# Bridging the last expert into the first dense tile with one-hot products, with wider row products and another split between VectorE and ScalarE

## The chip, the cores and the metric

One core of a Trainium2 chip runs the kernel. The metric is the device time of one launch in microseconds (us); the figure of a kernel is the median of its runs.

## The reference

Three layers run one after the other; all inputs are random, the dense weights come as 64-bit floats.

```
# 1: a complex decaying state, 4 batches x 8 heads x 768 steps, head size 48
a = a * min(|a|, 0.999) / (|a| + 1e-6)
S = a[t][:, None] * S + outer(k[t], v[t]);   y[t] = q[t] @ S.re
# 2: tokens x (3072 x 384); a token is computed if x @ w_skip > 0
e = argmax(x @ w_gate);   gate = softmax(x @ w_gate)[e]
x[token] += gate * (relu(x[token] @ w1[e]) @ w2[e])     # 8 experts, 384 -> 1024 -> 384
# 3: dense, 384 -> 2048 -> 384
h = x @ w_in;   out = max(0.01 * h, h) @ w_out
```

## The kernel before, in words

The batch is cut into two units of two batches (1536 tokens, `UT`). For each unit the work goes through the same stages:

1. *Rows* (`attention_rows`): on 128 rows (batch, head, chunk of 96 steps) VectorE normalises `a` (`norm`), runs the running product `P` step by step (`steps`: a product `t` and a sum `P` for each of the 96 steps, each needing the one before), and scales `q` and `k` by it (`scaled`). Steps come in blocks of 4 to 8 (unit 0) or 3 to 6 (unit 1). In unit 0 the order of a block on VectorE, ScalarE and TensorE is written out by hand: `timed` gives every instruction a place in the block from the `AT_...` lists, and the engines keep that order. Unit 0's products stay on the chip in two large tiles called `stash` (k and q).
2. *Chunks* (`attention_chunks`): 16 pairs of chunk and batch on TensorE. In unit 0 `columns` turns k's columns back into rows (`kps`, into `kqt`): the copy of one half of the heads goes to ScalarE, of the other to VectorE.
3. *Routing* (`Routing.part`, in two parts of 14 and 2 pairs): which 128 tokens each expert takes (`idx`), and their gates (`gsl`).
4. *Experts* (`Experts`): for each of 8 experts the tokens' rows are gathered from the DRAM buffer `xd` (`gathers`, one indirect DMA each), turned (`columns`), multiplied by `w1` (`first`, four groups), then by `w2` (`second`), gated and added to the token's row on VectorE (tile `xo`), and scattered back to `xd` by an indirect DMA on GpSimd.
5. *Dense* (`Dense`): tiles of 512 tokens (`TN`). `load` reads the tile's rows from `xd` into `xr` (SyncE's DMA queue), `columns` turns them by 12 TensorE transposes in three groups and splits each group into two fp16 halves (`xTh` by ScalarE, `xTl` by VectorE), `first` makes 16 slices of the hidden layer with 9 matmuls each, `second` makes the output. Two tiles run between unit 0's experts and unit 1's chunks.

Unit 1's rows (`behind`) and the conversion of the dense weights (`convert`) are fillers. A filler is a generator; `budget(gen, us, engines)` draws instructions from it until the costs that it yields reach `us`. `BG_CHUNK` is drawn at each of the 80 yields of unit 0's chunks, `BG_ROUTE` after the routing, and `BG_EXPERT` four times in each expert as long as the expert's number is below `LASTE`. `convert` takes `w_in` in 16 pieces: a piece of 64-bit words is loaded into one of two `raw` buffers (its DMA is issued when the piece before the last has been read), VectorE packs it in three instructions (`cst`), ScalarE makes the high half and VectorE the low half (`m2w`). `swap`, after expert 3's `first`, puts the conversion of `w_in` ahead of the rows in the experts' filler `feed`; what is left of it is run after the experts. `w_out` is converted while the first dense tile runs.

The program's scheduler may move an instruction ahead of others on its engine by its own estimate of when operands are ready. Where `keep("V")` (or A, T, G) is on, an instruction is instead queued behind the one that was written just before it on that engine. `budget(..., "VA")` turns this on for the filler's VectorE and ScalarE instructions in the experts; in the dense stage the rows are drawn without it. SyncE's DMA queue issues in order: an issue that has to wait holds those behind it.

A filler's cost for one instruction over n steps is `(70 + 1.04 * n * 48) / 1e3`, for one of a conversion `(70 + 1.04 * 384) / 1e3`.

## Time and profile before

| what | us |
|---|---|
| median of 3 runs (921.21 to 929.61) | 927.39 |
| profiled execution | 919.73 |
| its span | 917.6 |
| TensorE busy | 820.6 (89%) |
| VectorE busy | 608.4 (66%) |
| ScalarE busy | 502.4 (55%) |
| GpSimd busy | 140.5 (15%) |

The span is one execution from its first to its last instruction; times in the rows below are from the span's start. The profile gives the engines short names: PE is TensorE's matmul, PEld its weight load, DVE VectorE, ACT ScalarE, POOL GpSimd, SPq and ACTq the DMA queues of SyncE and ScalarE. "Busy" of an instruction runs from its start to its end, and two in a row can overlap.

In that execution unit 0's rows run until about 134 us, its chunks until about 215, the routing until 238, the experts until 328, then comes a gap on TensorE, then the two dense tiles from 346 to 480. Unit 1's chunks start at 480, its experts and the other dense tiles fill the rest.

### The profile page before, as it was taken

How to read it: one execution, taken by the hardware profiler on the slowest of the kernel's cores; microseconds unless marked ns; L12 is line 12 of the kernel's file. 1: busy time of each engine (PE TensorE's matmuls, PEld its weight loads, DVE VectorE, ACT ScalarE, POOL GpSimd, SP SyncE). 2: the span in 40 equal slices, each digit the busy share in tenths (PEclk: the TensorE clock that was granted, in tenths of full speed). 3: DMA queues.
4: the chain of work that ended last, by engine and by line, in shares of the span. 5: the costliest groups of instructions: out<-in, count | busy, mean ns of one | idle time of the engine just before them, and what ended most of it. 6: DMA issues, size and time to landing. Idle time of an engine off the chain costs nothing.

```text
span 917.6 us, 17826 instructions
## 1 busy us (share of the span) xinstructions
PE 820.6 (89%) x6674; PEld 569.8 (62%) x6674; DVE 608.4 (66%) x1534; ACT 502.4 (55%) x1071; POOL 140.5 (15%) x162
## 2 busy tenths in 40 slices
PE   2888878997699939999999979989999999999997
PEld 1666667997488814545569978547686546456454
DVE  6999974787999988999803654876676460450530
ACT  5789875675456445646507866565564350440530
POOL 9100012121714330000022111140111000000000
PEclk9999999999799978999999999999999999999999
DMA  5567536898589976364357995064773201000000
GB/s 153 149 173 197 158 101 192 261 271 283 191 283 331 321 230 223 105 207 136 95 146 185 247 260 153 21 206 154 242 238 111 85 5 57 10 1 26 9 10 28
DMA packets 126512, 143.61 MB, mean 157 GB/s; under 512 B 34058, under 2 KB 109514, under 8 KB 126416
## 3 DMA queue, kind: packets, MB, share of 16 engines
q1 hardware_dynamic: 113488, 120.46, 43.9%
q10 hardware_dynamic: 10880, 17.30, 5.8%
q0 software_dynamic: 2048, 4.61, 1.4%
q8 instruction: 54, 0.88, 0.4%
q14 instruction: 42, 0.34, 0.1%
HBM read 115.62 MB, written 28.41 MB: 157 GB/s over the span
## 4 chain that ended last, share of the span: by engine, by line
PE 52%; DVE 18%; DMA 15%; ACT 10%; issue 3%; SPq 1%; ACTq 0%; POOLq 0%; POOL 0%; DVEq 0%
PE ops L91 18%; PE hps L91 12%; PE yps L91 6%; PE sps L91 4%; DVE gg L91 4%; PE ad L91 3%; DVE cst L91 3%; DVE gl L91 3%; DMA cw<-in_moe_w_dram 2%; ACT gh L91 2%; PE tps L91 2%; DMA raw<-in_moe_w_in_dram 2%; DMA kqt<-kqd 2%; DMA vt<-vd 2%; PE ups L91 2%
## 5 line engine op out<-in xcount | busy, mean ns | idle before, releaser
L91 PE MATMUL hps<-xTh,m2w 128*128 128x512 f16 x576 | 173.8, 381 | 1.0 <-DVE gg L91 0.8
L91 PEld LDWEIGHTS <-m2w 128*128 128x128 f16 x864 | 84.6, 98 | 101.3 <-issue 4.4
L91 PE MATMUL ops<-m2w,gh 128*128 128x384 f16 x512 | 125.2, 326 | 0.0
L91 PE MATMUL hps<-xTl,m2w 128*128 128x512 f16 x288 | 109.4, 381 | 0.2 <-DVE xTl L91 0.2
L91 DVE TENSOR_TENSOR gg<-hps,gg 128x512 f32<-128x512 f32 x96 | 65.6, 684 | 65.2 <-ACT gg L91 64.9
L91 PE MATMUL ops<-m2w,gl 128*128 128x384 f16 x256 | 83.5, 326 | 0.0
L91 ACT ACTIVATE ot<-ops 128x384 f32<-128x384 f32 x24 | 11.6, 489 | 125.9 <-PE ops L91 125.9
L91 PEld LDWEIGHTS <-gh 128*128 128x128 f16 x512 | 50.1, 98 | 32.7
L91 ACT ACTIVATE gg<-hps 128x512 f32<-128x512 f32 x96 | 56.3, 587 | 20.7 <-PE hps L91 13.8
L91 PE MATMUL ops<-m2w,stash 128*128 128x384 f16 x384 | 65.3, 326 | 2.5 <-ACT m2w L91 1.7
L91 DVE TENSOR_TENSOR t<-P,a 128x192 f32<-128x192 f32 x190 | 66.5, 350 | 0.9 <-DVE kr L91 0.3
L91 DVE TENSOR_TENSOR gl<-gg,gh 128x512 f16<-128x512 f32 x64 | 44.2, 690 | 33.9 <-ACT gh L91 33.2
L91 DVE SCALAR_TENSOR_TENSOR w<-cw,w 128x768 f16<-128x768 f32 x64 | 59.7, 952 | 9.3 <-ACT w L91 8.4
L91 ACT ACTIVATE gh<-gg 128x512 f16<-128x512 f32 x64 | 40.2, 629 | 42.8 <-DVE gg L91 42.7
L91 ACT ACTIVATE w<-cw 128x768 f16<-128x768 f32 x64 | 53.0, 842 | 18.6 <-DMA cw<-in_moe_w_dram 16.1
L91 POOL TENSOR_SCALAR_AFFINE_SELECT sc<-sc 96x384 f32<-96x384 f32 x64 | 34.8, 552 | 159.9 <-ACT sc L91 159.5
L91 POOL DMA_INDIRECT xd<-xo,idx x16 | 35.3, 2204 | 155.0 <-DVE xo L91 113.0
L91 PEld LDWEIGHTS <-stash 128*128 128x128 f16 x384 | 37.5, 98 | 29.7 <-issue 5.1
L91 DVE TENSOR_TENSOR P<-t 128x96 f32<-128x96 f32 x190 | 48.0, 253 | 1.4
L91 PE MATMUL yps<-stash,hh 128*128 128x384 f32 x128 | 42.8, 487 | 0.0
L91 PE MATMUL yps<-sc,vt 128*64 128x96 f32 x512 | 41.6, 251 | 0.0
L91 ACT ACTIVATE hh<-hps 128x256 f32<-128x256 f32 (+1 forms) x64 | 23.7, 378 | 30.8 <-PE hps L91 26.2
(243 smaller groups left out, 1724.8 us busy)
## 6 DMA issues: line engine op xcount, KB each, us to landing
cw<-in_moe_w_dram SPq DMA_DIRECT2D x64, 384.0 KB
stash<-in_moe_w_dram ACTq DMA_DIRECT2D x16, 768.0 KB
stash<-in_moe_w_dram SPq DMA_DIRECT2D x16, 768.0 KB
kqt<-kqd SPq DMA_DIRECT2D x16, 576.0 KB
kqd<-kq SPq DMA_DIRECT2D x14, 576.0 KB
vd<-gv SPq DMA_DIRECT2D x32, 192.0 KB
vt<-vd SPq DMA_DIRECT2D x32, 192.0 KB
raw<-in_moe_w_in_dram SPq DMA_DIRECT2D x16, 384.0 KB
```

What stands on the lines that cost most here:

```text
L91: ins = getattr(self.engine, op)(*args, **kw)
```

## The change

- The first dense tile's rows are loaded after expert 6 (`tiles`), before expert 7's result is in `xd`. GpSimd and VectorE make a one-hot matrix of 128 slots by 512 tokens from expert 7's token list (an iota of 384 and one of 128 columns, two comparisons). Expert 7's gated result is first made alone (`yg`), `Dense.columns` accumulates on its transposes, now written as products with the identity, the product of `yg` with the one-hot matrix (two matmuls in each of the three groups), and only then the row sum `xo` is made and scattered. From expert 6 on the VectorE instructions of `second` keep the written order.
- `LASTE` goes from 7 to 8: expert 7 draws fillers too. What is left of `w_in`'s conversion keeps its order on VectorE.
- In unit 0's rows three products that were made in halves (two in `scaled`, one in `norm`) are made in one instruction each; `AT_NORM` and `AT_SCALED` lose the places of the halves.
- `columns` of unit 0's chunks copies both halves of `kps` by ScalarE.
- `BG_CHUNK` goes from 0.3 to 0.4, and while a routing part is being drawn in unit 0's chunks, the rows are not drawn after it.

```diff
-BG_CHUNK = 0.3
+BG_CHUNK = 0.4
-BG_EXPERT, LASTE = 2.0, 7
+BG_EXPERT, LASTE = 2.0, 8
-AT_NORM = (0.034, 0.118, 0.189, 0.26, 0.342, 0.381)
+AT_NORM = (0.034, 0.118, 0.189, 0.26, 0.381)
-AT_SCALED = (0.481, 0.525, 0.746, 0.75, 0.862, 0.93, 0.961)
+AT_SCALED = (0.481, 0.746, 0.75, 0.862, 0.93)
...
-            if stash:
-                V.tensor_tensor(kq[1][:, :, 0], kq2[:, 1], P[:, :, 0], ALU.mult)
-                yield cost(i)
-                V.tensor_tensor(kq[1][:, :, 1], kq2[:, 1], P[:, :, 1], ALU.mult)
-            else:
-                V.tensor_tensor(kq[1], both(kq2[:, 1], i), P, ALU.mult)
+            V.tensor_tensor(kq[1], both(kq2[:, 1], i), P, ALU.mult)
...
-                if a:
-                    V.tensor_copy(half, p)
-                else:
-                    A.activation(half, p, AF.Copy)
+                A.activation(o["kqt"][:L, 4 * a:4 * a + 4, 0, :], p, AF.Copy)
...
-        def second(self, e):
+        def second(self, e, early=None):
...
-            V.scalar_tensor_tensor(xo, yps, gsl[self.ui][:, e:e + 1], self.xg[e], ALU.mult, ALU.add)
+            keep("V" if self.place and e >= E - 2 else "")
+            if early:
+                yg = self.xp.tile([128, DM], F32, tag="xo", name="yg")
+                V.tensor_scalar(yg, yps, gsl[self.ui][:, e:e + 1], None, ALU.mult)
+                early(yg)
+                V.tensor_tensor(xo, yg, self.xg[e], ALU.add)
+            else:
+                V.scalar_tensor_tensor(xo, yps, gsl[self.ui][:, e:e + 1], self.xg[e], ALU.mult, ALU.add)
+            keep("")
             scatter(xd[self.ui], xo, idx[self.ui][:, e:e + 1], UT)
...
                 for s in range(4):
-                    T.transpose(tp_[:, s, :], self.xr[:, s, kk * 128:(kk + 1) * 128], ident)
+                    if late:
+                        T.matmul(tp_[:, s, :], self.xr[:, s, cs], ident, start=(s == 0), stop=False)
+                    else:
+                        T.transpose(tp_[:, s, :], self.xr[:, s, cs], ident)
+                for n, (ts, oh) in enumerate(late[1] if late else ()):
+                    T.matmul(tp_.rearrange("p s t -> p (s t)")[:, ts], late[0][:, cs], oh, start=False, stop=n > 0)
...
-            budget(first_of(todo + [gen]) if todo else gen, us, "VAT")
+            budget(first_of(todo + ([] if ck.stash else [gen])) if todo else gen, us, "VAT")
...
+    def tiles():
+        dense.extend(Dense(u, t, mlp2["x"], None if u or t >= ND else g) for u in range(NU) for t in range(UT // TN))
+        dense[0].load()
+        oh = [ex.xp.tile([128, DM], F32, tag=f"xg{i}", name="oh", bufs=1) for i in range(2)]
+        at = oh[1][:, TN - DM:TN - DM + 1]
+        V.tensor_copy(at, idx[0][:, E - 1:E])
+        for x, n, t in ((oh[0], DM, 0), (oh[1], TN - DM, DM)):
+            G.iota(x[:, :n], pattern=[[1, n]], base=t, channel_multiplier=0, allow_small_or_imprecise_dtypes=True)
+            V.tensor_scalar(x[:, :n], x[:, :n], at, None, ALU.is_equal)
+            late.append((slice(t, t + n), x[:, :n]))
+
+    then[E - 2, 1] = tiles
+    experts(ex, feed, BG_EXPERT, then=then, early=lambda yg: dense[0].columns((yg, late)))
...
+    keep("V")
     run(mlp2["conv", 0])
...
-    dense[0].load()
-    dense[0].columns()
```

## Rows read from the trace of the kernel before

**Rows 1.** By stretch: busy PE, PEld, DVE, ACT, POOL (instructions), clock, DMA share, GB/s

```profile
60.00:80.00 20.00, 16.97 (x126) 12.83 (x126) 19.69 (x59) 18.04 (x44) 0.00 (x0) 1.00 0.63 178
180.00:200.00 20.00, 20.00 (x314) 19.14 (x314) 16.00 (x47) 14.37 (x34) 4.84 (x8) 1.00 0.97 279
```

**Rows 2.** The chain that ended last, 282 to 352 us: start, us, what

```profile
288.14 6.24 DMA raw<-in_moe_w_in_dram
...
296.17 5.29 DMA raw<-in_moe_w_in_dram
...
335.29 6.47 DMA xd<-xo,idx
...
341.78 4.44 DMA xr<-xd
...
346.26 1.97 PE tp L91 x8
```

**Rows 3.** Timeline around the gap, all engines: start, us, what, wait and its releaser

```profile
314.31 1.60 SPq L859 DMA_DIRECT2D stash<-in_moe_w_dram  x2
...
321.04 0.61 DVE L91 SCALAR_TENSOR_TENSOR xo<-yps,gsl,xg 128x384 f32<-128x384 f32 x1
...
322.90 5.56 PE L91 MATMUL yps<-stash,hh 128*128 128x384 f32 x16
...
334.41 0.61 DVE L91 SCALAR_TENSOR_TENSOR xo<-yps,gsl,xg 128x384 f32<-128x384 f32 x1
...
335.29 4.35 POOL L91 DMA_INDIRECT xd<-xo,idx  x1 [10.93 <-DVE xo L91]
...
340.82 0.36 DVE L91 TENSOR_SCALAR cst<-raw 128x384 int32<-128x384 int32 x1 [1.51 <-DMA raw<-in_moe_w_in_dram]
```

**Rows 4.** Timeline, VectorE in one block of unit 0's rows: start, us

```profile
59.91 0.36 DVE L91 TENSOR_TENSOR t<-P,a 128x192 f32<-128x192 f32 x1
60.30 0.26 DVE L91 TENSOR_TENSOR P<-t 128x96 f32<-128x96 f32 x1
60.48 0.55 DVE L91 TENSOR_TENSOR pu<-ad,pg 128x384 f32<-128x384 f32 x1
60.95 0.35 DVE L91 TENSOR_TENSOR t<-P,a 128x192 f32<-128x192 f32 x1
61.21 0.55 DVE L91 SCALAR_TENSOR_TENSOR pu<-pu,pg 128x384 f32<-128x384 f32 x1
```

**Rows 5.** Timeline, VectorE in unit 1's rows and where the conversion of w_in starts

```profile
258.16 0.75 DVE L91 TENSOR_TENSOR a<-ari,nrr 128x576 f32<-128x576 f32 x1
258.83 0.35 DVE L91 TENSOR_TENSOR t<-P,a 128x192 f32<-128x192 f32 x1
...
267.38 0.75 DVE L91 TENSOR_TENSOR a<-ari,nrr 128x576 f32<-128x576 f32 x1
...
285.77 0.61 DVE L91 SCALAR_TENSOR_TENSOR xo<-yps,gsl,xg 128x384 f32<-128x384 f32 x1
286.30 0.35 DVE L91 TENSOR_SCALAR cst<-raw 128x384 int32<-128x384 int32 x1
```

**Rows 6.** Copies of the tile kps: ns min/median/max, first and last start

```profile
L91 ACT ACTIVATE kqt<-kps x16: 472/480/502, 135.6 to 213.9; 96x384 f32<-96x384 f32 x16
L91 DVE COPY kqt<-kps x16: 541/547/554, 136.3 to 215.7; 96x384 f32<-96x384 f32 x16
```

**Rows 7.** The scatters of xd alone: ns min/median/max, first and last start

```profile
L91 POOL DMA_INDIRECT xd<-xo,idx x16: 969/1318/8409, 260.3 to 711.6; - x16
```

**Rows 8.** The tile cst alone, 5 us stretch: DVE busy (instructions), ACT, clock, DMA, GB/s

```profile
385.00:390.00 5.00, 3.14 (x8) 1.05 (x2) 1.00 0.49 164
```

**Rows 9.** Waits between 346 and 482 us: in total, times, longest

```profile
PE ops L91 <- ACT m2w L91: 1.7, 1, 1.7
```

**Rows 10.** Timeline, end of unit 1's rows and start of its chunks

```profile
456.06 0.36 SPq L313 DMA_DIRECT2D kqd<-kq  x1
...
480.54 3.32 PE L91 MATMUL tps<-ident,kqt 96*96 96x96 f32 x32
```

More of the change, by code (lines that the diff above doesn't have):

```diff
@@ L243, in norm @@
             a4s[i] = a4
[L244 to L249 removed]
+            V.tensor_tensor(a4[:, :, 0::2, :], ari.rearrange("p c t d -> p t c d"), both(rr, i), ALU.mult)
             if i + 3 < nb and not (stash and i in MIRROR):
@@ L301, in scaled @@
             yield cost(i)
-            if stash:
-                V.tensor_tensor(kq[0][:, :, 0], kq2[:, 0], P[:, :, 0], ALU.mult)
-                yield cost(i)
-                V.tensor_tensor(kq[0][:, :, 1], kq2[:, 0], P[:, :, 1], ALU.mult)
-            else:
-                V.tensor_tensor(kq[0], both(kq2[:, 0], i), P, ALU.mult)
+            V.tensor_tensor(kq[0], both(kq2[:, 0], i), P, ALU.mult)
             if i + 2 < nb:
@@ L967, in load, with columns @@
                               .rearrange("(s p) c -> p s c", p=128))
-        def columns(self):
+        def columns(self, late=None):
             self.xTh = self.xp.tile([128, 3, TN], F16, tag="xTh", name="xTh2", bufs=1)
@@ L1160, in second_ff, with experts @@
                 yield 2
-    def experts(ex, behind, us, then={}, mixed=none):
+    def experts(ex, behind, us, then={}, mixed=none, early=None):
         if ex.place:
@@ L1258, in moe_attention_kernel @@
     then[3, 0] = swap
-    experts(ex, feed, BG_EXPERT, then=then)
+    room = stash[0].rearrange("p c b t -> p (c b t)").bitcast(F16)
+    g = [room[:, j * 16 * TN:(j + 1) * 16 * TN].rearrange("p (f t) -> p f t", f=16) for j in range(2)]
+    dense, late = [], []
+    def tiles():
[10 more added lines that the diff above has]
+    experts(ex, feed, BG_EXPERT, then=then, early=lambda yg: dense[0].columns((yg, late)))
     (wih, wil), (woh, wol), m2x = mlp2[0], mlp2[1], mlp2["x"]
@@ L1262, in moe_attention_kernel @@
     ex.xp.release()
+    keep("V")
     run(mlp2["conv", 0])
-    room = stash[0].rearrange("p c b t -> p (c b t)").bitcast(F16)
-    g = [room[:, j * 16 * TN:(j + 1) * 16 * TN].rearrange("p (f t) -> p f t", f=16) for j in range(2)]
-    dense = [Dense(u, t, m2x, None if u or t >= ND else g) for u in range(NU) for t in range(UT // TN)]
+    keep("")
     nd = len(dense) // NU
-    dense[0].load()
-    dense[0].columns()
     for _ in dense[0].first():
```

10 lines of the change are left out of this document (2 added, 8 removed).

## The prediction

> **What bounds the kernel now.** I read the busy time by stretch first, then the chain of waits over the gap between the experts and the dense tiles, then the timeline of VectorE and of SyncE's queue there. Three stretches are touched. In unit 0's rows VectorE is busy 19.69 of 20 us and TensorE is not: VectorE's order sets the pace [rows 1]. In unit 0's chunks TensorE is busy 20.00 of 20, VectorE has 4 us and ScalarE 5.6 us free, and the DMA engines are taken to 0.97 [rows 1]. Between experts and dense tiles TensorE has nothing from 322.90 + 5.56 = 328.46 to 346.26, 17.8 us [rows 2, 3]. The chain shows what fills it: expert 7's sum `xo` comes only at 334.41, though its operand was there at 328.46, its scatter takes 6.47, the load of `xr` 4.44 [rows 2, 3].
>
> Sums are made against the profiled execution, 919.73 us. The median of the runs is 7.66 above that; a difference worked out here is added to 927.39.
>
> **Unit 0's rows.** Three products a block go from two instructions to one. An instruction of 384 columns is followed by the next after 0.47 (60.48 to 60.95), one of 576 after 0.67 (258.16 to 258.83) [rows 4, 5]; on that line one of 768 takes 0.87. Six halves cost 2.82, three wide ones 2.61: 0.21 less. But the halves also stood between steps. A `t` followed by an independent instruction gives way after 0.26 (60.95 to 61.21), one followed by its own `P` after 0.39 (59.91 to 60.30) [rows 4]: 0.13 of waiting. By the places in the `AT_` lists the removed ones (0.342, 0.525, 0.961 of 16 step places: 5.5, 8.4, 15.4) were each the only VectorE work between two steps, so three more pairs touch: 3 x 0.13 = 0.39 more. Net +0.18 a block, ten blocks of eight steps: +1.8 us. Bounds: -2.1 (no new pair waits) to +2.5 (the four small blocks too). I take +1.8, since the pairs that touch today show the wait.
>
> The Trainium skill, page VectorE: DVE Perf Modes, section The DRAIN you can't avoid, says that the next instruction starts only when the pipe of the one before is empty, and its rules ask for few instructions. By that the change gains the lower bound, 2.1 us. The trace doesn't agree: the independent instruction at 61.21 starts 0.09 before `t` ends.
>
> **Unit 0's chunks.** VectorE loses 16 copies of 0.547, 8.8 us; ScalarE gains 16 of 0.480, 7.7 us, about one for each pair of the 16 [rows 6]. `BG_CHUNK` draws 0.1 more at 71 yields, 7.1 units of cost. A block of unit 1's rows is 7.6 units by the code (6 steps of 0.56, `norm` 1.78, `scaled` 2.45) and takes 9.2 us (258.16 to 267.38) [rows 5], so 7.1 units are 8.6 us of VectorE: it comes out even with the copies, under TensorE's 20.00. The cover is ScalarE's 5.6 free us in 20; both additions on it are about 3 us in 20. I take 0; the bounds are -1 (a product that waits for the slower copy today) and +7.7 (no ScalarE copy hidden), the latter a rival below. Drawing the routing part alone is worth nothing: the nine yields that are left hold 3.6 units, the part's own yields sum to 6.98, so the rows would have had no turn there before either.
>
> **The bridge.** It removes scatter and load of expert 7 from the path, 10.9 us, and lets TensorE go on as soon as `yg` and `xr` are there. What are they now behind? VectorE's kept order. Twelve draws of 2.0 after `swap` hold 24 units; a piece of `w_in` costs 1.69 (0.6 + 3 times 0.469), so expert 6's `xo` now stands behind the first two instructions of piece 14 (counted from 0), and `yg` behind all 16 pieces and 5 more units of rows, drawn by expert 7 (4 x 2.0 more; 32 - 27). Before, these sums could run ahead: expert 6's at 321.04, while piece 14 began at 340.82 [rows 3].
>
> So the pace of the pieces decides. They start behind expert 3's `xo`, at 286.30 [rows 5], and that is tied to TensorE. Two buffers make two chains; 14 pieces took 340.82 - 286.30 = 54.5 us, 7.8 a pair. A cycle is one load, 6.24 or 5.29 [rows 2], and the three readings, at 3.14 / 8 = 0.39 each [rows 8] 1.2, and the rest is unit 1's rows, which the scheduler put between them. These rows now wait: the ones drawn in expert 7 are kept behind the last piece, and all later ones need their `P`. A cycle becomes 5.77 + 1.2 = 7.0 while expert weights load, whose last issue ends at 315.9 [rows 3]; with one load's time behind it, I put that at 320. Later it is as for `w_out`, eight instructions, two pieces, in 5 us: 5.0 [rows 8]. Seven cycles: 33.7 us at 7.0 are 4.8 of them, 2.2 at 5.0 are 11: piece 14 starts at 331. Expert 6's `xo` is done 1.4 later, 332.4. Its scatter: this one held GpSimd 4.35 of its 6.47 [rows 2, 3], the median one 1.32 [rows 7], so 3.4 to 6.5; I take 3.4, since unit 1's row transfers stand still then. With 0.3 to issue and 4.44 for the load `xr` is there at 340.6. Piece 15 starts 2.5 after piece 14 and is done 2 later, 335.5; 5 units of rows at 9.2 / 7.6 are 6.1: `yg` at 341.6. That is 4.7 before today's 346.26.
>
> The one-hot products add 512 columns in each of three groups. A product of 384 columns takes 5.56 / 16 = 0.35, so 0.46 a group, 1.4 in all; at the rate of the first transposes after the gap, 1.97 / 8 for 128 columns, 3.0 [rows 2, 3]. I take 2.2. The transposes need `xr` alone and run ahead. Iotas, comparisons and the later scatter of expert 7 lie in GpSimd's and VectorE's free time before 331, or beside the first dense tile, whose successor needs `xr` much later: nothing. If SyncE's queue stands behind that scatter, only `w_out` loads wait. The conversion of `w_out` can begin earlier, as `w_in`'s ends at 335 and no more after 347; TensorE's wait for it, 1.7 [rows 9], goes. Bridge: -4.7 + 2.2 - 1.7 = -4.2.
>
> What is late next are unit 1's rows. Of the 55.3 us from 286.30 to 341.6 VectorE works 25 on pieces (64 instructions of 0.39), 6.1 on rows and about 4 on sums and comparisons: 20 idle, so at most 20 more than now, and it has 8.6 less to do. The rows end at most 11.4 after today's 456.06. Their write and the first load of `kqt`, taken as long as the longest transfer of the gap, 6.5 each, make 480.5; TensorE would want its chunks at 480.54 - 4.2 = 476.3 [rows 2, 10]. At the worst, then, this gives the 4.2 back; I take nothing, since VectorE waits now too (1.51 before piece 14 alone) [rows 3].
>
> Sum: +1.8 + 0 - 4.2 = -2.4, **925 us**. With its own bounds (rows -2.1 to +2.5, the scatter at 6.5 and the products at 1.4 or 3.0, some -5 to +2 on the bridge) it lies between 919 and 932.
>
> **Rivals.** *The bridge opens.* All loads take what `w_out`'s do, a cycle of 5.0: piece 14 starts at 321.3, `xr` is there at 331, the rows of expert 7 end at 332, TensorE resumes 14.3 earlier, less 2.2 and the 1.7 above in favour: -13.8, with +1.8 -12.0: 915. For it: fewer transfers compete. Against it: the two loads that the chain shows beside the weights took 5.29 and 6.24 [rows 2]. The Trainium skill, page DMA: Bandwidth & Descriptors, section Anatomy of one DMA, gives about 2.0 us and the bytes at 436 GB/s, for 393 KB an estimate of 2.9 us; with that the bridge would open. The trace disagrees in this stretch, with about twice that.
>
> *The wait moves into VectorE's queue, and the kernel is slower.* The loads don't speed up, a pair stays at 7.8: piece 14 starts at 340.8, expert 6's `xo` is done at 342.2, `xr` comes between 350 and 353.4, piece 15 is done at 346.7, the rows at 352.8. TensorE starts 6.7 later than today, and the one-hot products at the slow rate add 3.0: +9.7, with +1.8 +11.5: 939. It decides from where piece 14 starts after about 333.5: from there `yg`, 10.6 behind it, and 2.2 of products are past 346.26. For it: the forecast's 331 is close to that.
>
> *ScalarE fills up in the chunks.* The kept order of three engines lets one late ScalarE copy hold a product; 0.48 in each of 16 pairs, +7.7: 933. Against it: 5.6 free us in 20.
>
> **How the numbers follow.** Chances: forecast 0.43, open bridge 0.28, slower 0.18, ScalarE 0.11. About 1% is what a measurement of this kernel can tell from no change: 918.1 and 936.7. Faster: 0.20 of the open bridge's 0.28 and 0.10 of the forecast, whose lower end lies near the line, 0.30. Slower: 0.12 of the 0.18, 0.02 of ScalarE, 0.02 of the forecast, 0.16. Within: 0.54. The range takes in the open bridge nearly whole and the slower case at its price: 913 to 939.
>
> **What would show it.** In the trace after: no row instructions of unit 1 on VectorE among the `w_in` pieces; piece 14 near 331 (321 or 341 for the rivals); `yg` right behind rows, not right behind expert 7's last product; TensorE idle some 13 us there, not 3; a block of unit 0's rows longer by 0.2; chunks still with a full TensorE. The prediction is wrong if the pieces' loads are much faster or slower than 6 us, or if the scheduler finds other work for VectorE among them.

## The result and the profile after

The changed kernel takes 929.41 us (median of 18 runs, 924.50 to 934.62), the kernel before in the same series 923.11 us (median of 18, 915.86 to 929.61). The ratio is 1.0071, interval 1.0046 to 1.0095: slower by about 6 us, where 2.4 us faster was forecast. The profiled execution after has a span of 922.9 us, 5.3 more than before; it lies 4.5 us below the median of its kernel, the one before 3.4 below.

The order around the gap came out as the text forecast it, but later. First the timeline around the gap in the kernel after (start, us, what, wait and its releaser), which answers to [rows 3]:

```profile
288.09 0.35 DVE L91 TENSOR_SCALAR cst<-raw 128x384 int32<-128x384 int32 x1
...
298.88 0.36 DVE L91 TENSOR_SCALAR cst<-raw 128x384 int32<-128x384 int32 x1 [7.31 <-DMA raw<-in_moe_w_in_dram]
...
321.43 0.36 DVE L91 TENSOR_SCALAR cst<-raw 128x384 int32<-128x384 int32 x1 [2.60 <-DMA raw<-in_moe_w_in_dram]
...
336.45 0.36 DVE L91 TENSOR_SCALAR cst<-raw 128x384 int32<-128x384 int32 x1
...
337.32 0.61 DVE L91 SCALAR_TENSOR_TENSOR xo<-yps,gsl,xg 128x384 f32<-128x384 f32 x1
...
338.21 1.04 POOL L91 DMA_INDIRECT xd<-xo,idx  x1 [24.91 <-DVE xo L91]
...
347.60 0.61 DVE L91 TENSOR_SCALAR yg<-yps,gsl 128x384 f32<-128x384 f32 x1
...
348.14 2.07 PE L91 MATMUL tp<-ident,xr 128*128 128x128 f32 x8 [15.32 <-DMA xr<-xd]
...
355.27 0.38 PE L91 MATMUL hps<-xTh,m2w 128*128 128x512 f16 x1
```

The chain of waits of the kernel after at the same place, answering to [rows 2] (start, us, what):

```profile
338.21 3.82 DMA xd<-xo,idx
...
342.05 6.05 DMA xr<-xd
```

The rows at 288.09, 298.88, 321.43 and 336.45 are the pieces 0, 2, 8 and 14 of `w_in`. Piece 14 starts at 336.45, not 331; expert 6's `xo` stands right behind it, `xr` lands 10.2 us after that sum's end, and TensorE still idles 15.32 us. It resumes at 348.14; before it was 346.26 [rows 2].

VectorE, in the 60 us in which that happens, in the kernel before and then in the kernel after (a stretch: us, PE, PEld, DVE, ACT, POOL busy with instructions, clock, DMA share, GB/s):

```profile
280.00:340.00 60.00, 48.46 (x281) 37.19 (x280) 55.63 (x149) 29.96 (x74) 21.74 (x5) 0.93 0.91 304
```

```profile
280.00:340.00 60.00, 51.34 (x303) 39.38 (x301) 37.89 (x85) 18.59 (x47) 3.96 (x4) 0.98 0.87 286
```

VectorE's idle time went from 4.4 to 22.1 us. Most of it is waiting for the loads of the pieces, in nine waits (VectorE's wait from 286 to 340 us in the kernel after: us in total, times, longest):

```profile
DVE cst L91 <- DMA raw<-in_moe_w_in_dram: 20.1, 9, 7.3
```

Between the first and the last piece of `w_in` the kernel before makes 21 steps `P` of unit 1's rows, the kernel after none.

**Stage marks.** Executions of the same code reach the experts at different times: in the kernel before and in e3 and e4, which differ from it only behind that point, expert 0's first transpose on TensorE starts at 238.65, 238.10 and 244.81. So all marks below are counted from that transpose, in us (the profiled execution of each kernel); each but *end* is a start. *xo(6)*: expert 6's sum. *Resume*: the dense tile's first transpose. *Last tp*: its last group of transposes or one-hot products. *w_out*: the last piece of `w_out` on VectorE. *Rows*: the last step `P` of unit 1. *Chunks*: unit 1's first chunk product. The ratio has its 95% interval and is taken against runs of the kernel before in the same series. In the names, *free* means that the sums of `second` are not in the kept order, *three buffers* that the conversions have three `raw` buffers, each load issued two pieces ahead.

| kernel | start | xo(6) | resume | last tp | w_out | rows | chunks | end | ratio of times to before |
|---|---|---|---|---|---|---|---|---|---|
| before | 238.65 | 82.4 | 107.6 | 110.7 | 168.1 | 211.1 | 241.9 | 679.0 | 1 |
| after | 240.51 | 96.8 | 107.6 | 113.9 | 164.3 | 225.4 | 244.1 | 682.4 | 1.0071 (1.0046 to 1.0095) |
| e1 wide products alone | 240.77 | 82.4 | 107.6 | 110.6 | 167.7 | 210.7 | 241.5 | 684.8 | 0.9999 (0.9972 to 1.0027) |
| e2 chunk part alone | 242.92 | 83.2 | 107.9 | 110.9 | 167.3 | 192.1 | 241.3 | 681.2 | 1.0008 (0.9981 to 1.0035) |
| e3 bridge alone | 238.10 | 97.7 | 108.3 | 115.6 | 166.5 | 237.9 | 250.4 | 693.9 | 1.0102 (1.0054 to 1.0149) |
| e4 bridge, free, LASTE 7 | 244.81 | 84.6 | 96.6 | 107.4 | 174.3 | 221.9 | 246.8 | 681.9 | 1.0022 (0.9994 to 1.0050) |
| e5 after, three buffers | 239.53 | 92.0 | 102.9 | 109.2 | 153.5 | 219.3 | 237.9 | 675.3 | 0.9976 (0.9947 to 1.0004) |
| e6 after, free, LASTE 7 | 244.42 | 83.9 | 95.8 | 106.6 | 174.2 | 204.0 | 246.1 | 686.5 | 1.0066 (1.0033 to 1.0100) |
| e7 e6 with three buffers | 249.41 | 83.8 | 101.5 | 109.1 | 161.8 | 204.3 | 238.9 | 674.8 | 0.9957 (0.9926 to 0.9987) |
| e8 after, no products | 240.57 | 98.4 | 110.3 | 113.8 | 167.3 | 229.9 | 245.9 | 687.4 | 1.0041 (1.0002 to 1.0079) |
| e9 before, three buffers | 243.09 | 83.9 | 105.1 | 108.3 | 152.4 | 205.9 | 236.1 | 672.2 | 0.9953 (0.9926 to 0.9980) |
| e10 after, free, three buffers | 245.64 | 82.2 | 93.6 | 101.4 | 154.6 | 219.7 | 232.0 | 672.7 | 0.9974 (0.9948 to 1.0000) |
| e11 after, LASTE 7 | 247.27 | 103.5 | 114.1 | 120.8 | 183.6 | 188.9 | 254.7 | 694.6 | 1.0215 (1.0177 to 1.0253) |
| e12 e10, BG_CHUNK 0.5 | 248.20 | 81.2 | 94.2 | 107.6 | 155.1 | 213.7 | 236.2 | 672.0 | 0.9969 (0.9938 to 1.0000) |
| e13 e9, chunk part at 0.5 | 243.48 | 84.0 | 108.9 | 112.0 | 155.2 | 178.4 | 239.8 | 678.5 | 1.0027 (0.9992 to 1.0063) |
| e14 after, free | 246.56 | 83.2 | 93.6 | 103.0 | 168.8 | 228.7 | 242.6 | 684.1 | 1.0108 (1.0067 to 1.0148) |

(e8's last tp is the start of the last eight of its 24 products with the identity.)

The marks fit one reading of what the chunks of unit 1 wait for; it is taken from the sixteen rows, and the waits of TensorE below bear it out in part. They start about 128 to 132 us after the last tp, or 71 to 74 us after `w_out`'s last piece, or 12 to 14 us after the rows, whichever is latest. Before, the first two are level: 110.7 + 131.2 and 168.1 + 73.8 both give 241.9. By this reading a TensorE that resumes sooner in the kernel before gains next to nothing by itself: `w_out`'s pieces are the next bound, at no distance. In the kernel after it is the last tp (113.9 + 130.2), in e3 the rows (237.9 + 12.5), in e4 and e6 `w_out` (72.5, 71.9), in e14 `w_out` and the rows at once (73.8, 13.9), in e10 the rows (12.3), with the last tp close (130.6). In e11 it is `w_out` again (71.1), with the last tp late too.

From the chunks to the end the profiles scatter: 435.1 to 443.5 us over the sixteen, 437.1 in the kernel before and 443.3 in e1, whose program is the same there. So a few us at *end* say nothing, and what a mark is worth in time is read from the ratio alone.

### The profile page after: what moved, and what is told of

Read it like the earlier page. It is cut to its first block, busy times and chain, and to the rows that moved or that the text cites. A ratio compares the mean times of both kernels' runs of the same rounds, so it can differ in the third digit from the quotient of the medians.

```text
span 922.9 us, 17853 instructions
## 1 busy us (share of the span) xinstructions
PE 827.6 (90%) x6698; PEld 574.5 (62%) x6698; DVE 605.9 (66%) x1480; ACT 507.2 (55%) x1087; POOL 125.9 (14%) x164
## 4 chain that ended last, share of the span: by engine, by line
PE 54%; DVE 16%; DMA 14%; ACT 9%; issue 6%; SPq 1%; ACTq 0%; POOLq 0%; DVEq 0%; POOL 0%
PE ops L91 18%; PE hps L91 13%; PE yps L91 7%; PE sps L91 4%; DVE gg L91 3%; DMA xd<-xo,idx 3%; DVE gl L91 3%; DMA cw<-in_moe_w_dram 2%; PE tps L91 2%; PE ad L91 2%; ACT gh L91 2%; PE ups L91 2%; DVE cst L91 2%; DMA kqt<-kqd 1%; DMA raw<-in_moe_w_out_dram 1%
## 5 line engine op out<-in xcount | busy, mean ns | idle before, releaser
L91 ACT ACTIVATE ot<-ops 128x384 f32<-128x384 f32 x24 | 11.7, 491 | 118.0 <-PE ops L91 116.6
L91 POOL TENSOR_SCALAR_AFFINE_SELECT sc<-sc 96x384 f32<-96x384 f32 x64 | 37.0, 592 | 148.6 <-ACT sc L91 148.4
L91 POOL DMA_INDIRECT xd<-xo,idx x16 | 22.1, 1384 | 191.7 <-DVE xo L91 152.1
L91 PE MATMUL ad<-psq,ident 128*128 128x384 f32 (+2 forms) x48 | 22.2, 597 | 21.3 <-ACT psq L91 21.3
```

The lines of the kernel that those rows point to most:

```text
L91: ins = getattr(self.engine, op)(*args, **kw)
```

## The experiments

The theories: (1) VectorE's kept queue, paced by the loads of `w_in`, eats the bridge; (2) the chunk stage costs the time; (3) the one-hot products and the load of `xr` cost what the gap gives; and, added with the free orders, (4) TensorE comes sooner but the dense stage gives it back.

**e1, wide products alone**

```
-                V.tensor_tensor(kq[1][:, :, 0], kq2[:, 1], P[:, :, 0], ALU.mult)
-                V.tensor_tensor(kq[1][:, :, 1], kq2[:, 1], P[:, :, 1], ALU.mult)
+            V.tensor_tensor(kq[1], both(kq2[:, 1], i), P, ALU.mult)
...
```

> The kernel before with the wide row products alone (with the AT_ lists of the change). The prediction's step: a block of unit 0's rows 0.18 to 0.23 us longer, the rows end about 1.8 us later, the kernel 1.8 us slower, ratio 1.002. Rival (what the changed kernel's trace shows, first kps at 134.40 against 134.71): the rows wait for loads of a as well, these waits take the longer blocks in, and the kernel is the same within 0.5 us.

Measured 925.97 us against 926.19, ratio 0.9999. The interval, -2.6 to +2.5 us, holds both expectations: the term of +1.8 is not resolved. The block itself is longer, as forecast: from one `t` to the same one eight steps on e1 and the kernel after take 9.84 us, the kernel before 9.61.

**e2, the chunk part alone**

```
-BG_CHUNK = 0.3
+BG_CHUNK = 0.4
...
-                if a:
-                    V.tensor_copy(half, p)
-                else:
-                    A.activation(half, p, AF.Copy)
+                A.activation(o["kqt"][:L, 4 * a:4 * a + 4, 0, :], p, AF.Copy)
```

> The kernel before with both copies of kps on ScalarE and BG_CHUNK 0.4 alone. Theory 1 (the loss is in the kept queue of VectorE around the bridge): chunks and routing within 2 us, the kernel -1 to +2 us. Theory 2 (the chunk stage costs it: the copies on ScalarE and the earlier transfers of unit 1's rows collide with the stage's own): the experts start 2 to 4 us later, expert 0's gather lands late, the kernel 3 to 6 us slower.

Measured 926.93 against 926.19. Theory 2's 3 to 6 us are outside the interval except for its lower end (up to +3.2 us). Something of it is there: TensorE's wait just before expert 0 is 7.0 us here. With two `raw` buffers it is 5.8 to 5.9 in the four kernels with BG_CHUNK 0.3 (before, e1, e3, e4) and 6.6 to 7.4 in the six with 0.4 (7.4 in the kernel after): the part costs 0.7 to 1.6 us there. Whether the experts start later by more than that stays open: they start at 244.1 in the mean of nine kernels with 0.4, at 241.1 in five with 0.3, with spreads of 10 and 7 us. The rows end 19 us sooner, which is worth nothing while the chunks wait for something else.

TensorE's waits from 215 to 250 us in e2, and in e1 (who waited for whom: us in total, times, longest):

```profile
PE tp__3571 L91 <- DVE nrr L91: 7.0, 1, 7.0
```

```profile
PE tp__3472 L91 <- DVE nrr L91: 5.9, 1, 5.9
```

**e3, the bridge alone**

```
-BG_EXPERT, LASTE = 2.0, 7
+BG_EXPERT, LASTE = 2.0, 8
...
+            keep("V" if self.place and e >= E - 2 else "")
+            if early:
...
+    then[E - 2, 1] = tiles
```

> The kernel before with the bridge alone: early load, one-hot products, LASTE 8, kept VectorE order around it; rows, kps and BG_CHUNK as before. Theory 1 (expert 6's sum, expert 7's gated result and ScalarE's relu stand in the kept queues behind w_in's pieces): xo of expert 6 behind piece 14 at 332 to 338, TensorE takes up the dense tile at 343 to 349, experts end 1 to 3 us later, the kernel +1 to +5 us. Theory 2 (the chunk stage costs it, the bridge is worth its -4): 3 to 5 us faster. Theory 3 (the one-hot products and the load of xr cost as much as the shorter gap gives back): the same within 1 us, with xr landing by 340 and 4 us more of products than of transposes.

Measured 934.02 against 926.19, +7.8 us, more than theory 1 said. The resume is at 108.3, level with before; what is worse is the dense stage. Timeline of e3, resume and start of unit 1's chunks:

```profile
346.40 1.01 PE L91 MATMUL tp<-ident,xr 128*128 128x128 f32 x3 [17.59 <-DMA xr<-xd]
...
488.48 0.76 PE L91 MATMUL tps<-ident,kqt 96*96 96x96 f32 x7 [2.08 <-DMA kqt<-kqd]
```

TensorE's waits in e3 between these two (345 to 489 us):

```profile
...
PE tp L91 <- DVE xTl L91: 2.9, 1, 2.9
...
PE ops L91 <- ACT m2w L91: 1.1, 1, 1.1
```

The chunks start 8.5 us later than before. By parts, the last tp is 4.9 later, the second dense tile's transposes wait 2.9 for VectorE's split (not at all before), the chunks 2.1 for rows that ended 27 us later, and the waits for converted pieces are 1.2 shorter. So the bridge is the part that costs. In the kernel after the rows end 12.5 us sooner than in e3, since the chunk part drew more of them early, and the wait for them is gone; but the intervals of the two ratios overlap, and between e4 and e6, below, the ratios go the other way. What the chunk part is worth beside the bridge is not shown.

**e4, the bridge in free order** (the edit against e3)

```
-BG_EXPERT, LASTE = 2.0, 8
+BG_EXPERT, LASTE = 2.0, 7
...
-            keep("V" if self.place and e >= E - 2 else "")
+            keep("")
```

> The bridge alone, but with LASTE 7 as before (expert 7 draws no fillers) and without the kept VectorE order in second for experts 6 and 7, so that expert 6's sum and expert 7's gated result may go ahead of the conversion pieces. Theory 1: expert 6's sum runs near 321 as in the kernel before, xr lands near 330, the gated result comes 1 us behind expert 7's last product, TensorE takes up the dense tile at 333 to 336 instead of 346; less 2 to 3 us of one-hot products and what the later rows give back: 5 to 9 us faster than before. Theory 3 (the products and the load eat the gain): within 2 us of e3. Theory 4 (TensorE comes earlier but unit 1's rows end too late for its chunks): dense tile early, the start of unit 1's chunks within 2 us of the kernel before, the kernel the same.

Measured 927.77, +1.6 us; theory 1's price of 5 to 9 us faster is refuted. Its mechanism held: expert 6's sum comes at 84.6 and TensorE resumes 11.7 us sooner than in e3. But unit 1's chunks start 4.9 us later than before, and the kernel is no faster: theory 4's outcome, though not by its cause, since the rows end 24.9 us before the chunks. TensorE's waits from 340 to 500 us in e4:

```profile
PE ops L91 <- ACT m2w L91: 5.8, 2, 3.6
PE tp L91 <- DMA xr<-xd: 4.0, 1, 4.0
```

The wait for `xr`, 17.8 before, has become 4.0, and that for converted pieces has grown from 1.7 [rows 9] to 5.8. The last `w_out` piece comes 6 us later than before. The waits are only part of what is given back. TensorE from the resume to unit 1's chunks, in the kernel before, the kernel after and e4:

```profile
346.26:480.54 134.28, 131.81 (x697) 69.98 (x698) 105.89 (x250) 66.24 (x135) 6.82 (x9) 0.98 0.48 150
```

```profile
348.14:484.62 136.48, 134.19 (x721) 72.98 (x721) 118.41 (x290) 73.77 (x153) 12.41 (x16) 0.99 0.48 149
```

```profile
341.42:491.57 150.15, 141.04 (x721) 75.86 (x722) 118.45 (x276) 70.60 (x145) 14.01 (x16) 0.93 0.52 158
```

e4 takes 15.9 us more than before. 6.6 are waits (9.1 against 2.5). Behind them TensorE is granted the lower of its two clock levels again (1.2 of 2.4 GHz, in the rows a clock of 0.50): after a wait of 2.26 us that ends at 391.25 the granted clock is 0.50 from 391.85 to 395.25, and from 419.20, within a wait of 3.6 us that ends at 420.5, until 425.95. Over the stretch it is 0.934 (0.977 before), an estimate of 9.9 us lost against 3.0. The other 2.4 are TensorE's own added work.

**e5, the changed kernel with three raw buffers**

```
+NRAW = 3
...
-                    t4 = ep.tile([R, 2, 2, D], F32, tag="t4", name="t4", bufs=3)
+                    t4 = ep.tile([R, 2, 2, D], F32, tag="t4", name="t4", bufs=2 if ui else 3)
...
-            raw[j] = pool.tile([128] + shape + [2], I32, tag="raw", name="raw")
+            raw[j] = pool.tile([128] + shape + [2], I32, tag="raw", name="raw", bufs=NRAW)
...
-            if j + 1 < n:
-                load(j + 1)
+            if j + NRAW - 1 < n:
+                load(j + NRAW - 1)
...
-            x = self.xp.tile([128, 2, 3, 128], F16, tag="xT", name="xT_")
+            x = self.xp.tile([128, 2, 3, 128], F16, tag="xT", name="xT_", bufs=1)
```

The room for the third buffer comes from two others (`t4` in unit 1's rows, `xT_`), so this edit is not the third buffer alone.

> The changed kernel with three raw buffers for w_in's and w_out's conversion instead of two, so that each load is issued two pieces ahead (room for it: two t4 buffers instead of three in unit 1's rows, one buffer for the turned token rows). Theory 1 (the kept queue of VectorE goes at the pace of the raw loads): three chains, a pair of pieces takes 4.6 to 5 us instead of 6.9, piece 14 starts at 322 to 326, xr lands by 334, TensorE takes up the dense tile at 334 to 338 instead of 348, VectorE idles less than 10 us in 280 to 340 instead of 22, unit 1's rows end some 10 us earlier: 6 to 10 us faster than the changed kernel, 0.2 to 0.6% faster than the kernel before. Theory 2 (the DMA engines are the bound there, their share is 0.94 to 0.97 before 320): the loads take 8 to 9 us each instead of 6, the pieces keep 6.9 a pair, or the expert weights come late and TensorE waits for them: within 2 us of the changed kernel.

Measured 922.00, ratio 0.9976; by the two ratios 0.9% below the changed kernel. Sums and resume come 4.8 and 4.7 us sooner after the experts' start than in the kernel after, unit 1's chunks 6.2. The time is as theory 1 said. The pieces did not reach the 4.6 to 5 us a pair that it gave: the 15 intervals took 45.0 us, 6.0 a pair. (The 6.9 a pair that it takes for the kernel after is a mean of 8.3 and 5.0; see below.)

```profile
342.39 1.01 PE L92 MATMUL tp<-ident,xr 128*128 128x128 f32 x3 [11.88 <-DMA xr<-xd]
```

**e6 and e7, the changed kernel in free order, with two and with three buffers**

```
-BG_EXPERT, LASTE = 2.0, 8
+BG_EXPERT, LASTE = 2.0, 7
...
-            keep("V" if self.place and e >= E - 2 else "")
+            keep("")
...
(e7: and the edit of e5)
```

> The changed kernel with LASTE 7 and without the kept VectorE order in second: expert 6's sum and expert 7's gated result may go ahead, rows go between the pieces again; the rest of the change (copies on ScalarE, BG_CHUNK 0.4, wide products) stays. Theory 1: VectorE idles 4 to 8 us in 280 to 340 instead of 22, TensorE takes up the dense tile 6 to 9 us sooner after the experts' start than in the changed kernel, unit 1's rows end 10 to 14 us earlier: 0.5 to 1% faster than the changed kernel, at or below the kernel before. Theory 4 (TensorE then waits for w_in's and w_out's pieces, as in the bridge alone with free order, where these waits were 6 us): half of it is given back in the first dense tile, the kernel within 0.3% of the kernel before.

> Both: the free order with LASTE 7, and three raw buffers. Theories 1 and 4: w_in's pieces no longer hold TensorE in the first dense tile (waits for m2w under 2 us instead of 6), TensorE takes up the dense tile at 333 to 338, 7 to 12 us faster than the kernel before. Theory 2 (DMA the bound): like the free order alone, the conversion waits stay.

e6: 931.48, ratio 1.0066, no better than the changed kernel, though TensorE resumes 11.8 us sooner. Both theories failed in size: all of it, not half, is given back. `w_out`'s last piece is at 174.2, and the chunks follow it by 71.9. e7: 922.04, ratio 0.9957. With three buffers the last piece is at 161.8 and the chunks start 7.2 us sooner than in e6, although the resume is 5.7 us later. TensorE waits 2.2 us for `m2w`, where under 2 was expected, but the kernel is 4 us faster than before, not 7 to 12.

**e8, without the one-hot products**

```
...
-                for n, (ts, oh) in enumerate(late[1] if late else ()):
-                    T.matmul(tp_.rearrange("p s t -> p (s t)")[:, ts], late[0][:, cs], oh, start=False, stop=n > 0)
```

> The changed kernel without the six one-hot products: expert 7's result is not added into the first dense tile's columns (its tokens there miss that expert), all else stays. It measures the products and the wait for the gated result by themselves. Prediction's term: 2.2 us (bounds 1.4 to 3.0). By the trace of the changed kernel the products are on the path for 1.7 + 1.0 + 1.0 us and xr lands before the gated result is there: 3 to 4 us faster than the changed kernel if nothing behind them gives it back; 0 to 1 us if the dense tile waits for converted pieces or for unit 1's rows anyway.

Measured 929.58, ratio 1.0041; against 1.0071 the intervals overlap, so 3 us less is possible and not shown. In its profile `xr` landed later (resume 110.3), which hides the effect. The trace gives the size of the term by itself: from the first transpose to the dense tile's first matmul e8 takes 4.79 us (350.84 to 355.63), the kernel after 7.13 (348.14 to 355.27): 2.3 us for the products. 144 products into the hidden layer the difference is the same (35.65 and 38.00 us after the resume).

```profile
350.84 4.95 PE L91 MATMUL tp<-ident,xr 128*128 128x128 f32 x24 [17.90 <-DMA xr<-xd]
...
355.63 0.38 PE L91 MATMUL hps<-xTh,m2w 128*128 128x512 f16 x1
```

**e9, the kernel before with three raw buffers**

The edit is that of e5, on the kernel before: the third buffer, and the two others cut to make room.

> The kernel before with three raw buffers (and the same room for them: two t4 buffers in unit 1's rows, one buffer for the turned token rows). It separates the third buffer from the bridge. Theory 1 (the third buffer pays because the kept queue stands at the pace of the loads): in the kernel before the sums run ahead of the pieces, TensorE waits for scatter and load of the last expert, so the resume stays 106 to 108 us after the experts' start and the kernel is within 2 us of the kernel before. Rival (the third buffer pays by itself, by the w_out pieces or fewer conflicts in the dense stage): 3 us or more faster, and the bridge adds nothing.

Measured 919.04 against 923.84, ratio 0.9953. The rival holds, theory 1's expectation is wrong: the edit pays without the bridge, and the kernels with both (e5, e7, e10) are no faster than it. By which of its ways the third buffer pays, the rival left open, and no run separates them. The stretch from the first to the last `w_in` piece, in the kernel before, the kernel after and e9:

```profile
286.30:347.39 61.09, 43.29 (x261) 34.14 (x261) 53.67 (x142) 27.45 (x66) 26.09 (x11) 0.87 0.88 294
```

```profile
288.09:339.32 51.23, 43.24 (x260) 33.41 (x259) 30.01 (x63) 13.77 (x34) 3.96 (x4) 0.99 0.85 283
```

```profile
291.28:338.89 47.61, 42.21 (x255) 33.10 (x254) 45.19 (x119) 22.87 (x55) 24.31 (x5) 0.98 0.97 317
```

After took 10 us from this stretch by taking the rows out of it; VectorE does 30.01 us of work in 51.23. e9 makes it shorter still with 15 steps of the rows in it, VectorE busy 45.19 of 47.61. Its last `w_out` piece comes 15.7 us sooner than before, and its rows 5.2.

**e10 and e14, free sums with LASTE 8, with three and with two buffers**

```
-            keep("V" if self.place and e >= E - 2 else "")
+            keep("")
...
(e10: and the edit of e5)
```

> The changed kernel with three raw buffers and without the kept VectorE order in second, LASTE 8 kept: expert 6's sum goes two pieces earlier, expert 7's gated result ahead of the rows, but the rows still don't run between the pieces, so that the scatters stay near 1 us of GpSimd. Theory 1: expert 6's sum at 325 to 328 instead of 331.5, xr lands 4 to 6 us sooner than with three buffers alone, TensorE takes up the dense tile 97 to 100 us after the experts' start instead of 103: 0 to 4 us faster than three buffers in the kept order. Theory 4 (what the opened gap gives is given back in the dense tile, which waits for converted pieces and VectorE's splits): the same within 2 us.

> The changed kernel with two raw buffers and without the kept VectorE order in second; LASTE 8 stays. Theory 1: expert 6's sum runs behind piece 9 (82 to 86 us after the experts' start instead of 97), xr lands 10 us sooner, TensorE takes up the dense tile 95 to 99 us after the experts' start instead of 107.6, the late pieces then hold it (w_in's last piece at 98 to 100): half comes back, 2 to 5 us faster than the changed kernel. Rival (order without effect; loads alone count): within 2 us of the changed kernel, resume at 105 to 108.

e10: 920.74, ratio 0.9974. e14: 933.08, ratio 1.0108. Both resume at 93.6, 14 us sooner than before, as theory 1 said of e14; that it would be 2 to 5 us faster than the changed kernel failed: it is slower in the medians, with intervals that overlap. e10 resumes 9.3 us sooner than e5 and has its time (0.9974 and 0.9976), as theory 4 said. With the same resume, the edit of e5 puts unit 1's chunks at 232.0 instead of 242.6. TensorE in a late stretch of the dense tiles in e14, then its waits there (340 to 500 us):

```profile
400.00:420.00 20.00, 13.72 (x55) 6.09 (x54) 17.79 (x47) 7.63 (x16) 0.00 (x0) 0.83 0.51 167
```

```profile
PE ops L91 <- ACT m2w L91: 4.9, 4, 2.6
...
PE ops L91 <- DVE m2w L91: 2.2, 5, 1.2
```

and the same two views of e10:

```profile
400.00:420.00 20.00, 20.00 (x121) 11.55 (x119) 20.00 (x55) 12.25 (x28) 0.00 (x0) 1.00 0.60 190
```

```profile
PE tps L92 <- DMA pb<-ped: 2.5, 1, 2.5
PE tps L92 <- DMA kqt<-kqd: 1.6, 1, 1.6
```

In e14 the dense tile starves for `w_out`'s pieces (13.72 of 20 us busy, and the granted clock falls to 0.83). In e10 that is gone, and the chunks wait for unit 1's rows instead: they end 13.8 us later than in e9.

**e11, the changed kernel with LASTE 7 alone**

```
-BG_EXPERT, LASTE = 2.0, 8
+BG_EXPERT, LASTE = 2.0, 7
```

> The changed kernel with LASTE 7 alone: expert 7 draws nothing, so its gated result stands right behind expert 6's sum and ahead of the last piece and of the rows. The prediction put that wait (5 units of rows) on the path. Theory 1 (xr's landing, behind expert 6's kept sum, sets the resume, and the products wait for it): resume and unit 1's start within 1.5 us of the changed kernel, the kernel within 2 us of it. Rival (the rows ahead of the gated result are the wait): products 4 to 6 us sooner after the experts' start, the kernel 3 us or more faster than the changed one.

Measured 942.63 against 923.84, ratio 1.0215: neither expectation. With fewer fillers drawn, rows run between the pieces again (piece 14 starts 54.1 us after the first, 7.7 a pair), while the kept order still holds expert 6's sum behind piece 14:

```profile
350.74 0.61 DVE L91 SCALAR_TENSOR_TENSOR xo<-yps,gsl,xg 128x384 f32<-128x384 f32 x1
...
361.37 1.01 PE L91 MATMUL tp<-ident,xr 128*128 128x128 f32 x3 [22.17 <-DMA xr<-xd]
```

The sum is done at 351.35, the resume is 10.0 us later, as in the kernel after. Free the same kernel (e6) and the sum comes 19.6 us sooner and the kernel is 1.5% faster. Here the kept order by itself is what costs.

**e12 and e13, rows drawn earlier, with the bridge and without**

```
-BG_CHUNK = 0.4
+BG_CHUNK = 0.5
...
(e12: on e10; e13: on e9, from 0.3 to 0.5, with both kps copies on ScalarE)
```

> The kernel of three raw buffers and free sums (LASTE 8, bridge) with BG_CHUNK 0.5 instead of 0.4: 7 units more of unit 1's rows are drawn in unit 0's chunks, some 8.6 us of VectorE. If unit 1's rows give back what the bridge opens: they end some 8 us sooner after the experts' start, the waits of unit 1's chunks for kqt and pb (4.1 us) go, its chunks start 2 to 4 us sooner, the kernel 3 to 6 us faster than with 0.4, 0.6 to 0.9% faster than the kernel before, if the chunks of unit 0 still cover the draw. Rival (the chunks' cover is used up): the experts start later by up to 8 us and nothing is won. Rival (the rows are not what gives it back): waits gone, the time the same.

> The kernel before with three raw buffers, both kps copies on ScalarE and BG_CHUNK 0.5, without the bridge and the wide products: the control of e12. Unit 1's rows ended 30 us before its chunks there, so rows drawn earlier should be worth at most 1 us by the dense stage's freer VectorE: within 2 us of three buffers alone (0.5% faster than the kernel before). If e12 is faster than this by 3 us, that is what the bridge is worth once neither the loads nor the rows hold it; if not, the bridge's products and its later rows cost what it opens.

e12: 922.71, ratio 0.9969. The rows end 6 us sooner after the experts' start and the chunks' waits are gone, but the time is that of e10: the second rival. In the profile `yg` came late in their place: TensorE waited 5.7 us for it.

```profile
350.09 1.65 PE L92 MATMUL tp<-oh,yg 128*128 128x384 f32 x2 [5.74 <-DVE yg L92]
```

e13: 927.84, ratio 1.0027, 0.7% above e9, not within 2 us. Its rows end 27.5 us sooner than e9's, and the experts' scatters fall among their transfers: the one for expert 5 holds GpSimd 10.87 us, expert 6's starts 6.18 behind it and holds 4.53, and the last expert's, whose sum starts at 338.21, cannot start until 345.47.

```profile
317.56 10.87 POOL L92 DMA_INDIRECT xd<-xo,idx  x1 [10.35 <-DVE cst L92]
...
334.61 4.53 POOL L92 DMA_INDIRECT xd<-xo,idx  x1 [6.18 <-DVE m2w L92]
...
345.47 0.97 POOL L92 DMA_INDIRECT xd<-xo,idx  x1 [6.33 <-DVE t L92]
...
352.38 0.90 PE L92 MATMUL tp<-ident,xr 128*128 128x128 f32 x3 [17.51 <-DMA xr<-xd]
```

The bridge takes just this scatter off the path. Here, beside e13, it goes with 0.6% (0.9969 against 1.0027; same series, means 5.1 us apart, 95% interval 2.2 to 8.0; e12 has the wide products too). Beside e9 it is worth nothing. No version was faster than e9, the kernel before with a third raw buffer.

## Why the prediction was wrong

**The bridge, -4.2: this step failed.** The order of events was as forecast, but three of its terms were not: the pace of the first pieces was too fast, scatter and load too short, and part of TensorE's new work was put at nothing.

*The pace of the pieces.* Forecast were 44.7 us from the first piece to piece 14, at 7.0 a pair until 320 and 5.0 afterwards. Measured are 48.4 (288.09 to 336.45). The 5.0 came as forecast: from piece 8 on three pairs take 15.02. The 7.0 did not: the first four pairs take 33.34 (288.09 to 321.43), 8.3 each, and in the kernel before, with rows among them, 30.75 (286.30 to 317.05), 7.7 each. So taking the rows out shortened nothing there; the forecast had put what was above one load and its readings down to rows. It had named loads much slower than 6 us as a sign of being wrong, and this sign came: piece 2, whose load is issued at 289.66, is read at 298.88, after 9.2 us. The two halves in the kernel after:

```profile
288.09:321.43 33.34, 31.85 (x195) 25.05 (x195) 16.06 (x35) 9.01 (x23) 2.92 (x3) 1.00 0.96 319
321.43:336.45 15.02, 11.39 (x67) 8.36 (x65) 11.57 (x24) 4.18 (x10) 0.00 (x0) 1.00 0.70 232
```

VectorE is idle half of the first. e3 and e8, in the same order, take 32.2 and 33.4 for it. The DMA engines are taken to 0.96 there and to 0.70 behind it (0.97 in the kernel before from 286.30 to 319.64); that they set this pace is argued from these shares, and not shown. In all piece 14 is 3.7 late.

*Scatter and load.* They took 10.2 after the sum, not 8.2 (`xr` alone 6.05, with 4.44 before): 2.0. The first piece starts 1.8 later, since the experts start 1.9 later. Together 7.5, and 340.6 + 7.5 is the 348.1 at which `xr` was there. Counted from the experts' start the resume is level with before (107.6): of the -4.7 nothing is left.

The Trainium skill, page DMA: Bandwidth & Descriptors, section Anatomy of one DMA, has a fit for transfers that GpSimd issues, some 2.0 us and the bytes at 436 GB/s. Taken for the load of `xr`, which SyncE issues, as the prediction took it for the raw loads, it gives an estimate of 3.8 us for the 786 KB; by that it would have landed 2.3 us sooner. The trace disagrees, with 6.05 beside the raw loads.

*TensorE's work.* The products, +2.2, measure 2.3 (e8). But the transposes of this tile are now products with the identity, and there are 24 of them (e8's row) where the kernel before has 12 transposes:

```profile
346.26 1.97 PE L91 MATMUL tp<-ident,xr 128*128 128x128 f32 x8 [17.80 <-DMA xr<-xd]
...
349.30 1.06 PE L91 MATMUL tp<-ident,xr 128*128 128x128 f32 x4
```

The prediction gave that nothing. Its size is an estimate. From the resume to unit 1's chunks TensorE is busy 131.81 us before and 134.19 after (the two rows under e4). Part of that is the clock: behind the gap, idle for 17.80 and 15.32 us, TensorE is granted 0.50, the 1.2 GHz level, for the first 6.04 us before and the first 3.64 after:

```profile
346.26:352.30 6.04, 6.04 (x21) 3.69 (x22) 4.58 (x11) 2.84 (x5) 0.00 (x0) 0.50 0.94 304
```

```profile
348.14:351.78 3.64, 3.64 (x13) 3.03 (x14) 2.75 (x8) 0.52 (x1) 0.00 (x0) 0.50 0.41 131
```

At this level the same work takes twice as long (in the kernel after eight products with the identity take 1.87 us from 348.14, and 0.93 from 351.71), so half of it is lost, 3.0 and 1.8 us. The work went from 128.8 to 132.4: 3.6 more, 2.3 for the one-hot products, and the rest, over 1 us, for the doubled transposes. The shorter stretch at the lower level took 1.2 off again; the prediction didn't count on that.

*The waits.* The -1.7 came: TensorE's waits for converted pieces, 2.3 us before (1.7 [rows 9] and 0.6 for VectorE's half), are 0.2. In their place the second dense tile's transposes wait 2.0 for VectorE's split. TensorE from 346 to 500 us in the kernel after:

```profile
PE tp L91 <- DVE xTl L91: 2.0, 1, 2.0
PE ops L91 <- ACT m2w L91: 0.2, 1, 0.2
```

So from the resume to the chunks 3.6 more work, 1.2 less for the clock and 0.2 less waiting make the 2.2 us by which the chunks are late.

*The order was right.* The rows left the stretch of the pieces, the sum stood behind piece 14, and the resume followed the end of the sum by 10.0 to 11.2 us wherever the order was kept (after, e3, e5, e8, e11). The rival "the wait moves into VectorE's queue" had the right place and side. Pieces at 7.8 a pair, its condition, are nearly those of e11 (7.7), with rows among them: 18.8 us slower than before, where the rival had 11.5.

*What is late next.* In the changed kernel itself neither `w_out`'s pieces nor unit 1's rows hold the chunks (79.8 and 18.7 us ahead of them). But they decide what mending the pace would give. The text took nothing for unit 1's rows, and let `w_out`'s conversion begin earlier for a gain. VectorE's idle time was forecast well (20 us; 22.1 in 60). But the work that it left undone had to be done in the dense stage, where VectorE is busy nearly all the time (19.2 to 20.0 us of each 20 from 355 to 455): the rows ended 14.3 us later against the experts' start, more than the 11.4 that the text put as the most, and in e3, without the earlier draw, 26.8. And `w_out`'s pieces, dismissed as a wait of 1.7, were level with the resume in the kernel before. What the rival "the bridge opens" forecast for the resume came in e14, e4 and e6, 11 to 14 us sooner, by the free order and not by faster loads. Its -13.8 was given back in full, in waits, in the lower clock behind them and in the added products (e4): no kernel with two buffers and the bridge is faster than before.

**The experts, taken as untouched,** were not quite: with the pieces' work unmixed, ScalarE's `relu` of the last experts stands behind late `m2w`. TensorE's weight load waits for it from 300 to 335 us in the kernel after:

```profile
PEld yps L91 <- ACT hh L91: 3.5, 4, 1.6
```

Expert 7's products start 2.5 us later than before after the experts' start. It cost nothing here, since the resume waited for `xr`.

**Unit 0's rows, +1.8:** the block grew by 0.23 us (0.18 forecast), for the reason given, three more pairs of `t` and `P` that touch. The kernel after, VectorE in a block, answering to [rows 4]:

```profile
58.24 0.95 DVE L91 TENSOR_TENSOR qr<-kq,P 128x768 f32<-128x768 f32 x1
59.11 0.35 DVE L91 TENSOR_TENSOR t<-P,a 128x192 f32<-128x192 f32 x1
59.50 0.26 DVE L91 TENSOR_TENSOR P<-t 128x96 f32<-128x96 f32 x1
```

`P` starts 0.39 after `t`; the wide product gives way after 0.87. Whether the stage is longer by 1.8 is not resolved (e1); in the profiles unit 0's last `P` starts at 129.6 after and 129.9 before. The gain of 2.1 that the prediction worked out from the Trainium skill's page VectorE: DVE Perf Modes, section The DRAIN you can't avoid, is not there: the block got longer with fewer instructions. That section of the Trainium skill also says that an instruction that is not held starts earlier, which the prediction left out; the trace agrees with that, with the next start 0.87 behind that of an instruction of 0.95.

**The chunks, 0:** the part alone is within -1.8 and +3.2 us of before, and its one visible price is TensorE's wait ahead of expert 0, 0.7 to 1.6 us longer (e2). TensorE stays nearly full in it, as the stretch of the kernel after shows that answers to [rows 1]:

```profile
180.00:200.00 20.00, 19.43 (x298) 18.15 (x298) 15.45 (x45) 15.19 (x38) 6.42 (x8) 1.00 0.96 268
```

Drawing the routing part alone does nothing, as forecast: with that line as before, the program has the same instructions in the same order on every engine.

**The sum.** The profiled execution is 5.3 us longer: 1.9 ahead of the experts (1.6 of it TensorE's longer wait before expert 0, 7.4 against 5.8), 2.2 from there until unit 1's chunks, and 1.2 behind them, less than the scatter of that stretch. The medians differ by 6.3. That 929.41 lies within the text's own 919 to 932 is luck: the kernel before measured 923.11 in this series, not the 927.39 that the sum started from, and against it the change is 6.3 slower, outside the 4.6 that these bounds allow. That the bridge is what costs is shown by e3 beside e1 and e2; how its price divides over the stages rests on one profile of each kernel.

## What to carry to other kernels

Before an engine's gap is closed, work out the time of each of its other inputs at the far end of the next stage; here, by the marks, the gap on TensorE was level with `w_out`'s conversion, and with two buffers no shorter gap paid (e4, e6, e14). Work that is put in a kept order behind a filler goes at the filler's pace; where that filler waits for loads, taking other work out from between its pieces need not speed it up (8.3 a pair after, 7.7 before, in the first half). And other work that used that engine's waits is pushed into the next stage: count the engine's busy time over both stages, not over the gap. When a paced filler is on such a path, try a further buffer for its loads first; in this kernel that edit, with two other buffers cut for it, gave 0.5% (0.2 to 0.7) and the bridge on top of it nothing.

## What the runs showed of the hardware

The scatter's hold on GpSimd depends on what else moves. Where unit 1's rows stood still (after, e3, e5, e10, e14) it was 0.97 to 1.04 us for the last experts; where they ran between the pieces, up to 11.03 (e4). That the rows' transfers cause it is argued from this, and not shown by itself. The longest one, in e4's timeline:

```profile
319.29 11.03 POOL L91 DMA_INDIRECT xd<-xo,idx  x1 [7.62 <-DVE xo L91]
```

Waits inside the dense stage cost more than their length: in e14 TensorE was busy 13.72 us of 20 at a granted clock of 0.83, where e10 had 20.00 at 1.00. In e4 the clock behind such waits was 0.50 for 3.4 and 6.75 us.
